# Second MLP product of token tiles 0 to 7 by seven block products in place of eight

## The chip, the cores and the metric

The kernel runs on one core of a Trainium2 chip. The core has a matrix engine (PE in the profile, with its weight loads shown apart as PEld), a vector engine (DVE), a scalar engine (ACT), a general engine (POOL, nearly idle here) and SP, whose queue issues most of the DMA transfers. Each engine works through its own instructions in the order in which the program lists them, and semaphores hold an instruction back until the instructions it depends on are done. The metric is the device time of one execution in microseconds; lower is better.

## What is computed

The reference normalises the 2048 tokens of x (512 features), sends them through an attention block with cached keys and values (32 heads of 128) and, beside it, through a gated MLP branch, and multiplies the two:

```python
xn = _layernorm(x, axis=-1)
s = _A_ref(xn, A_k_cache, A_v_cache, A_wq, A_wo)          # softmax attention, output projection
g = _silu(_B_ref(xn, B_w1, B_w2, B_w3, B_w4))
return x + s * g
# in _B_ref: hs = shifted gelu(layernorm(x) @ w1) @ w2;  x1 = x + hs
#            h2 = _gelu(_layernorm(x1) @ w3) @ w4;       return x1 + h2
```

The change concerns the last product alone, `gelu(...) @ w4`: 2048 tokens by 1792 hidden features, times 1792 by 512.

## The kernel before

All token work is in 16 tiles of 128 tokens. `xall` holds the running MLP state of all tiles in bf16, `h2T` the gelu output with the hidden features on the partitions, so that a block of 128 hidden features by 128 tokens can be a stationary operand as it lies.

The MLP branch runs first, in about the first 118 us; the attention loop over 128 units (head, quarter of the queries) follows and takes nearly all of the rest. Two functions carry the second MLP. `m3(c, f)` (line 286) makes two blocks of hidden features (f) for a chunk c of four token tiles: eight matmuls of 512 columns into a PSUM tile of two banks and one gelu on ACT over 1024 columns. `m4(t, ps, ...)` (line 295) makes the product of one token tile with `w4`: 14 matmuls of 512 columns, one for each block of hidden features, summed in one PSUM bank. `gate_out(t)` (line 815) wraps it: `m4`, then `x2` (line 301, DVE adds the bank to `xall`), `gate_tanh` (line 304, ACT) and `gate_silu` (line 309, DVE).

The order written out at lines 795 to 828 is: the 14 loads of `w4`, loads of the first keys and values mixed with `m3(0, ...)`, `m3(1, ...)` and the normalisations `ln2`, and then tiles 0 to 3 by `gate_out`, `m3(2, ...)`, tiles 4 to 7 by `gate_out`, `m3(3, ...)`. Tiles 8 to 15 (`held`, line 849) are worked off a few matmuls at a time inside the attention loop and are not touched by the change, beyond the names of their operands.

`pin` keeps every engine's instructions in the order of the text. On the SP queue the order around the change is: 14 loads of `w4` (line 796), keys and values of head 0, four transposes of `ln2(8)` to `ln2(11)`, keys and values of head 1, four transposes of `ln2(12)` to `ln2(15)` (line 284), keys and values of heads 2 and 3, four loads of `wo`.

Tiles of memory come from pools. A tag names a group of buffers of one size: `bufs=5` under tag `xi` means five of them, taken by each new tile in the order in which they came free; a new tile's first writer waits until all that read or wrote the buffer's last tile is done, transfers included. Line 171 takes from tag `xi`: for the input tiles 0 to 4, and in `ln2` for the normalised tiles with even t, which are read by the transposes of line 284:

```python
        y = token(t % 2 == 0, "xn2")
        norm_to(y[:], xall[:, t, :], mv2, rs2, t)
        pin(nc.sync.dma_start_transpose(out=xn2T[c][:, :, ts * P:(ts + 1) * P], in_=y[:]))
```

In PSUM, tag `ps_o` has two banks, `xa` and `xm` one each, and `ps_s` two tiles of two banks. Accesses of different engines to one PSUM tile are ordered by bank: a matmul that writes one half of a bank waits for an engine that reads the other half, and the other way round. The kernel has one block scheme of seven products already, for the queries (`product`, `q_take`, `q_part`, lines 367 to 423).

Of the kernel before, what the change touches and what calls it, by code (L numbers as in the profile page):

```python
# [8 lines left out]
ACT = mybir.ActivationFunctionType  # L9
ALU = mybir.AluOpType  # L10
FP32 = mybir.dt.float32
BF16 = mybir.dt.bfloat16
# [5 lines left out]
def kernel(  # L18
# [15 lines left out]
    nc = tc.nc  # L34
    P = nc.NUM_PARTITIONS
# [3 lines left out]
    Sq, D = x2d.shape  # L39
    _, H, Sk, Dh = A_k_cache.shape  # L40
# [5 lines left out]
    DC = D // P  # L46
    KC = Sk // P
    FC = F // P
# [11 lines left out]
    PADW = 8  # L60
    PSUM = bass.MemoryType.PSUM
    pin = tc.keep_in_program_order

    def pool(name, bufs=1, space=None, **kw):
        if space is not None:
            kw["space"] = space
        return tc.tile_pool(name=name, bufs=bufs, **kw)
# [4 lines left out]
    xall = const.tile([P, NT, D], BF16, name="xall")  # L72
# [22 lines left out]
    psO = ent(pool("psO", 2, PSUM))  # L95
    psX = ent(pool("psX", 1, PSUM))
# [4 lines left out]
    pR = right.enter_context(pool("pR", side="right", reuse_waits="tile"))  # L101
    left = ExitStack()
    pL = left.enter_context(pool("pL", reuse_waits="tile"))
# [7 lines left out]
    def mm(out, lhsT, rhs, start, stop, **kw):  # L111
        pin(nc.tensor.matmul(out=out, lhsT=lhsT, rhs=rhs, start=start, stop=stop, **kw))  # L112
# [8 lines left out]
        out=ident[:], in0=diag[:], scalar1=0.0, scalar2=None, op0=ALU.is_equal))  # L121
# [47 lines left out]
    def token(early, name):  # L169
        if early:  # L170
            return pL.tile([P, D], BF16, tag="xi", bufs=5, name=name)
        return tokp.tile([P, D], BF16, tag="ta", bufs=6, name=name)
# [9 lines left out]

    w1_sb = pL.tile([P, DC, D], BF16, name="w1_sb")
    w2_sb = pL.tile([P, DC, D], BF16, name="w2_sb")
    w3_sb = [pL.tile([P, DC, 2 * P], BF16, name=f"w3_sb{i}") for i in range(FC // 2)]
    hT = pL.tile([P, DC, Sq + PADW], BF16, name="hT")
    xn2T = {}
    w4_sb = [pR.tile([P, D], BF16, name=f"w4_sb{i}") for i in range(FC)]  # L190
    h2 = {}

    def power(out, ve):
# [92 lines left out]
    def m3(c, f):  # L286
        ps = psS.tile([P, 2, 512], FP32, name="ps_s")
        for j in range(2):
            for dc in range(DC):
                mm(ps[:, j, :], w3_sb[f][:, dc, j * P:(j + 1) * P], xn2T[c][:, dc, :],  # L290
                   dc == 0, dc == DC - 1)
        h2[c, f] = pR.tile([P, 2, 512], BF16, tag="h2T", bufs=FC, name="h2T")
        pin(nc.scalar.activation(out=h2[c, f][:], in_=ps[:], func=ACT.Gelu_apprx_tanh))  # L293

    def m4(t, ps, fcs):
        c, ts = divmod(t, 4)
        for fc in fcs:
            mm(ps[:], h2[c, fc // 2][:, fc % 2, ts * P:(ts + 1) * P], w4_sb[fc][:],
               fc == 0, fc == FC - 1)

    def x2(t, ps):
        pin(nc.vector.tensor_tensor(out=xall[:, t, :], in0=ps[:], in1=xall[:, t, :], op=ALU.add))

    def gate_tanh(t):
        th = token(False, "th")
        pin(nc.scalar.activation(out=th[:], in_=xall[:, t, :], func=ACT.Tanh, scale=0.5))
        return th

    def gate_silu(t, th):
        pin(nc.vector.scalar_tensor_tensor(  # L310
            out=xall[:, t, :], in0=th[:], scalar=1.0, in1=xall[:, t, :], op0=ALU.add, op1=ALU.mult))
# [29 lines left out]
    def x_block(qt, half, dcs):  # L341
        c = qt * 512 + 256 * half
        return xnT[:, dcs, c:c + 256]
# [23 lines left out]
    def product(v, k):  # L367
        g, qt, hh = units[v]
        h = g * HG + hh
        s = sw.setdefault(v, {})  # L370
        if k in (1, 7):
            s["ps"] = psX.tile([P, 2, 256], FP32, tag="xa", name="ps_q")
        w, o = wc[h], [wc[h][:, i] for i in range(4)]
        b11, _, b21, b22 = (wqs[h + j][:, d, :] for d in (LO, HI) for j in (0, 1))
        side, x, b = {
            1: (0, x_block(qt, 0, LO), b11),
            2: (0, x_block(qt, 0, HI), b21),
            3: (1, xs[qt, 3], b22),
            4: (0, x_block(qt, 1, HI), o[3]),
            5: (1, xs[qt, 0], o[0]),  # L380
            6: (1, xs[qt, 1], o[1]),
            7: (0, xs[qt, 2], o[2]),
        }[k]
        for dc in range(2):
            mm(s["ps"][:, side, :], b[:, dc, :], x[:, dc, :], k in (1, 7) and dc == 0, True, skip_group_check=True)
# [296 lines left out]
    for jc in range(DC):  # L682
        b = BASE_J[jc]
# [109 lines left out]
        elif t < 13:  # L793
            ln2(t - 5)
    for i in range(FC):
        pin(nc.sync.dma_start(out=w4_sb[i][:], in_=B_w4[i * P:(i + 1) * P, :]))
    for t in range(8, 12):
        stats(xall[:, t, :], mv2, rs2, t)
    for h in range(HG):
        load_k(h, range(KSPLIT))  # L800
        load_v(h, (0, 1))
        if h == 0:
            for f in range(FC // 2):
                m3(0, f)
            for t in range(12, 16):
                stats(xall[:, t, :], mv2, rs2, t)
            for t in range(8, 12):
                ln2(t)
        if h == 1:
            for f in range(FC // 2):  # L810
                m3(1, f)
            for t in range(12, 16):
                ln2(t)

    def gate_out(t):
        ps = psO.tile([P, D], FP32, tag="ps_o", name="ps_o")
        m4(t, ps, range(FC))
        x2(t, ps)
        gate_silu(t, gate_tanh(t))

    for t in range(0, 4):
        gate_out(t)
    for f in range(FC // 2):
        m3(2, f)
    for t in range(4, 8):
        gate_out(t)
    for f in range(FC // 2):
        m3(3, f)
    left.close()
    pB = left.enter_context(pool("pB", reuse_waits="tile"))  # L830

# [5 lines left out]
    for g in range(NG - 1):  # L837
        b = (g * QT + QT - 1) * HG
# [18 lines left out]
    def held_mm(n):  # L857
        for _ in range((4, 10)[n] if n < 2 else 3 if n < SPU + 2 else 2 if n < 2 * SPU else 1 + (n % SPU in (1, 5, 7))):
            if not held:
                return  # L860
            t, fc = held.popleft()
            if fc == 0:
                heldps[t] = psX.tile([P, 512], FP32, tag=("xa", "xm")[t % 2], name="ps_m")
            m4(t, heldps[t], (fc,))
            if fc == FC - 1:
                held_out(t, n)
# [34 lines left out]
    for v in pairs:  # L901
        a = (v - 2) * SPU
# [19 lines left out]
    for h in range(HG, H, 2):  # L922
        u = (h // HG) * QT * HG + (-4, -2)[h % HG // 2]
# [8 lines left out]
    for n in range(UB * SPU):  # L932
        u, p = divmod(n, SPU)
# [72 lines left out]
    n = UB * SPU  # L1006
    t0 = 4 * (QT - 1)
    ps, tb, yl, whole = {}, {}, {}, {}
# [25 lines left out]
    def pv_to(k):  # L1034
# [29 lines left out]
        out=diag[:], in0=diag[:], scalar1=0.0, scalar2=None, op0=ALU.is_equal))  # L1064
# [98 lines left out]
```

## Time and profile before

| | |
|---|---|
| median of 3 runs | 1236.7 us (1235.96 to 1236.73) |
| profiled execution | 1236.42 us, of which 1234.6 us from the first to the last instruction |
| PE busy | 1227.5 us of the span, 6267 matmuls |
| DVE busy | 1030.1 us, 1647 instructions |
| ACT busy | 1105.8 us, 1237 instructions |
| tiles 0 to 3 by `gate_out` | first matmul at 69.53 us |
| `m3(2, ...)` | first matmul at 81.62 us |
| tiles 4 to 7 by `gate_out` | first matmul at 93.70 us |
| `m3(3, ...)` | first matmul at 105.79 us |

The profiled execution is 0.28 us under the median. Times in the profile count from the first instruction. Matmuls are pipelined: one of 512 columns is listed with 379 ns, but in a row of them the next starts long before the last has ended, so that the cost of a stretch is read from the starts. In a group, "idle before" is the time that the engine stood before these instructions, with what ended most of it.

### The profile page before, as it was taken

Reading aid. Unit: us, or ns where it says so; the run is one execution under the profiler, and the core shown is the slowest. Engines: PE = TensorE matmul, PEld = TensorE weight load, DVE = VectorE, ACT = ScalarE, POOL = GpSimd, SP = SyncE. Lnnn points to the kernel's source line nnn. Section 1 sums busy time; section 2 is a strip of 40 time slices with the busy share of each in tenths; the row PEclk is TensorE's granted clock in tenths of the full one; section 3 lists DMA queues with packets and bytes.
Section 4 is the critical chain, followed back from the end, with each engine's and each line's share of the span. In section 5 each row is a group of like instructions: output and inputs, shape, how many; then the busy total and the mean of one; then the engine's idle time right before and its main releaser. Section 6 shows DMA issues by size and latency. Waiting matters only on the chain.

```text
span 1234.6 us, 17534 instructions
## 1 busy us (share of the span) xinstructions
PE 1227.5 (99%) x6267; PEld 636.5 (52%) x6267; DVE 1030.1 (83%) x1647; ACT 1105.8 (90%) x1237; POOL 26.6 (2%) x75
## 2 busy tenths in 40 slices
PE   9999999999999999999999999999999999999998
PEld 6444444455555555555555555555555555555545
DVE  7712778899888888988889888888889999999997
ACT  6345999899999999999999999999999999999996
POOL 5300000000000000000000000000000000000000
PEclk9999999999999999999999999999999999999999
DMA  8661122664334423354243523543345424553342
GB/s 176 168 140 35 31 39 65 96 99 94 63 80 100 106 57 82 87 111 85 58 95 91 111 56 69 103 104 72 76 83 111 107 58 90 99 107 66 77 81 66
DMA packets 244056, 107.75 MB, mean 87 GB/s; under 512 B 194816, under 2 KB 227712, under 8 KB 243968
## 3 DMA queue, kind: packets, MB, share of 16 engines
q1 hardware_dynamic: 243408, 106.17, 41.5%
q8 instruction: 49, 0.80, 0.3%
q10 hardware_dynamic: 560, 0.46, 0.1%
q14 instruction: 39, 0.32, 0.1%
HBM read 67.50 MB, written 2.36 MB: 57 GB/s over the span
## 4 chain that ended last, share of the span: by engine, by line
PE 94%; DVE 3%; DMA 2%; ACT 1%; issue 0%; SPq 0%; DVEq 0%; ACTq 0%
PE ps_s L112 39%; PE ps_o L112 37%; PE ps_wo L112 8%; PE ps_q L112 8%; PE ps_m L112 2%; DMA tT<-acc 1%; DVE acc L447 1%; ACT pT L436 1%; DMA rb<-dr 0%; DMA xin<-in_A_x_dram 0%; DVE sm L485 0%; PE ps_oh L112 0%; DVE oT L509 0%; DVE acc L451 0%; DVE y L1025 0%
## 5 line engine op out<-in xcount | busy, mean ns | idle before, releaser
L436 ACT ACTIVATE pT<-ps_s 128x1024 bf16<-128x1024 f32 x1016 | 1016.2, 1025 | 56.8 <-PE ps_s L112 26.1
L112 PE MATMUL ps_s<-qT,kT 128*128 128x512 bf16 (+1 forms) x2064 | 609.3, 378 | 0.0
L112 PE MATMUL ps_o<-pT,vb 128*128 128x512 bf16 x1984 | 590.2, 379 | 0.0
L447 DVE TENSOR_TENSOR acc<-acc,pT 128x2048 bf16<-128x2048 bf16 x254 | 307.0, 1208 | 54.9 <-ACT pT L436 54.4
L112 PEld LDWEIGHTS <-kT 128*128 128x128 bf16 x2064 | 232.7, 113 | 151.3 <-issue 1.0
L112 PEld LDWEIGHTS <-vb 128*128 128x128 bf16 x1984 | 193.9, 98 | 216.6
L442 DVE TENSOR_TENSOR acc<-pT 128x2048 bf16<-128x2048 bf16 x127 | 155.4, 1224 | 38.4 <-ACT pT L436 35.5
L112 PE MATMUL ps_wo<-wo_h,oT 128*128 128x512 bf16 x496 | 186.3, 379 | 0.0
L451 DVE TENSOR_TENSOR acc<-acc 128x1024 bf16<-128x1024 bf16 x127 | 87.4, 688 | 2.5
L509 DVE TENSOR_TENSOR oT<-ps_o,rb 128x512 bf16<-128x512 f32 x127 | 86.6, 682 | 1.1 <-DMA rb<-dr 0.8
L485 DVE TENSOR_REDUCE sm<-tT 128x4 f32<-128x512 bf16 x124 | 83.9, 676 | 2.8 <-DMA tT<-acc 2.7
L112 PEld LDWEIGHTS <-oT 128*128 128x128 bf16 x528 | 51.4, 98 | 52.6 <-issue 0.6
L112 PEld LDWEIGHTS <-wc 128*128 128x128 bf16 x440 | 43.0, 98 | 54.1 <-issue 2.7
L571 DVE TENSOR_TENSOR sacc<-ps_wo,sacc 128x512 f32<-128x512 f32 x96 | 65.7, 684 | 0.0
L112 PEld LDWEIGHTS <-wq_h 128*128 128x128 bf16 x398 | 38.9, 98 | 46.3
L112 PE MATMUL ps_q<-xnT,wq_h 128*128 128x256 bf16 (+1 forms) x288 | 61.1, 298 | 0.4 <-DVE sacc L559 0.4
L421 DVE TENSOR_TENSOR qT<-ps_q,tq 128x512 bf16<-128x512 f32 x55 | 38.0, 692 | 23.3 <-PE ps_q L112 22.9
L455 DVE TENSOR_TENSOR acc<-acc 128x512 bf16<-128x512 bf16 x127 | 52.9, 417 | 0.5
L293 ACT ACTIVATE h2T<-ps_s 128x1024 bf16<-128x1024 f32 x28 | 28.6, 1023 | 25.9 <-PE ps_s L112 25.9
L112 PE MATMUL ps_s<-xn2T,w_sb 128*128 128x512 bf16 x224 | 48.8, 379 | 0.0
L112 PEld LDWEIGHTS <-w_sb 128*128 128x128 bf16 x368 | 33.5, 98 | 29.6
L112 PE MATMUL ps_q<-xs,wc 128*128 128x256 bf16 x246 | 47.0, 273 | 0.0
(102 smaller groups left out, 585.6 us busy)
## 6 DMA issues: line engine op xcount, KB each, us to landing
rb<-dr SPq DMA_DIRECT2D x127, 256.0 KB, 3.9
vb<-in_A_v_cache_dram SPq DMA_DIRECT2D x62, 256.0 KB, 3.0
wq_h<-in_A_wq_dram SPq DMA_DIRECT2D x32, 128.0 KB, 3.0
wo_h<-in_A_wo_dram SPq DMA_DIRECT2D x32, 128.0 KB, 2.5
w_sb<-in_B_w_dram SPq DMA_DIRECT2D x8, 256.0 KB, 5.0
kT<-in_A_k_cache_dram SPq DMA_TRANSPOSE x128, 2.8
xl<-in_A_x_dram SPq DMA_DIRECT2D x16, 128.0 KB, 3.0
dr<-rc SPq DMA_DIRECT2D x127, 2.0 KB, 1.4
```

What stands on the lines that cost most here:

```text
L112: pin(nc.tensor.matmul(out=out, lhsT=lhsT, rhs=rhs, start=start, stop=stop, **kw))
L293: pin(nc.scalar.activation(out=h2[c, f][:], in_=ps[:], func=ACT.Gelu_apprx_tanh))
L421: pin(nc.vector.tensor_tensor(out=s["q"][:, 1:3], in0=ps, in1=u.to_broadcast([P, 2] + list(u.shape[2:])), op=ALU.add))
L436: pin(nc.scalar.activation(out=s["pT"][-1][:, jj:jj + 2, :], in_=sps[:], func=ACT.Exp, scale=SCALE))
L442: pin(nc.vector.tensor_tensor(out=s["acc"][:], in0=s["pT"][0][:], in1=s["pT"][1][:], op=ALU.add))
L447: pin(nc.vector.tensor_tensor(out=a[:], in0=a[:], in1=st[u]["pT"][i][:], op=ALU.add))
L451: pin(nc.vector.tensor_tensor(out=a[:, 0:2, :], in0=a[:, 0:2, :], in1=a[:, 2:4, :], op=ALU.add))
L455: pin(nc.vector.tensor_tensor(out=a[:, 0, :], in0=a[:, 0, :], in1=a[:, 1, :], op=ALU.add))
L485: pin(nc.vector.tensor_reduce(out=sm[:], in_=s["tT"][:], axis=mybir.AxisListType.X, op=ALU.add))
L509: pin(nc.vector.tensor_tensor(out=to, in0=o, in1=rb, op=ALU.mult))
L571: pin(nc.vector.tensor_tensor(out=sa, in0=ps[:], in1=sa, op=ALU.add))
```

## The change

For two token tiles at a time, the hidden features are split into even and odd blocks of 128 (seven each), the rows of `w4` with them, and the 512 output columns into halves. The product of a pair is then two by two blocks times two by two blocks, and these are multiplied by seven block products and sums of blocks (the Winograd form of Strassen's scheme). Each block product is seven matmuls of 256 columns. Four differences of blocks of `w4` are made once (`w4t`), four sums and differences of blocks of the hidden state for each pair (`h_sums`), both on DVE; `pair_out` holds the seven products and eight sums on the output side, one copy on ACT among them. `w4_sb` and `h2` become one tile each (per chunk), so that even and odd blocks can be addressed by one instruction.

The new tiles sit in buffers that earlier tiles have left: `w4t` in that of `hT`, the operand sums of a pair in the four buffers `xp` or in those of `w1` and `w2`, and the temporaries of 256 columns in the five buffers `xi`. The first pair of a chunk uses PSUM tag `xa` and the second `xm`; both use the two banks `ps_o`. The gates of a first pair are issued inside the second pair, behind its copy on ACT and ahead of its first sum on DVE.

```diff
-    w1_sb = pL.tile([P, DC, D], BF16, name="w1_sb")
-    w2_sb = pL.tile([P, DC, D], BF16, name="w2_sb")
+    w1_sb = pL.tile([P, DC, D], BF16, tag="w1", bufs=1, name="w1_sb")
+    w2_sb = pL.tile([P, DC, D], BF16, tag="w2", bufs=1, name="w2_sb")
...
-    hT = pL.tile([P, DC, Sq + PADW], BF16, name="hT")
+    hT = pL.tile([P, DC, Sq + PADW], BF16, tag="hT", bufs=1, name="hT")
...
-    w4_sb = [pR.tile([P, D], BF16, name=f"w4_sb{i}") for i in range(FC)]
+    w4_sb = pR.tile([P, FC // 2, 2, D], BF16, name="w4_sb")
...
-        h2[c, f] = pR.tile([P, 2, 512], BF16, tag="h2T", bufs=FC, name="h2T")
-        pin(nc.scalar.activation(out=h2[c, f][:], in_=ps[:], func=ACT.Gelu_apprx_tanh))
+        if f == 0:
+            h2[c] = pR.tile([P, FC // 2, 2, 512], BF16, tag="h2T", bufs=2, name="h2T")
+        pin(nc.scalar.activation(out=h2[c][:, f], in_=ps[:], func=ACT.Gelu_apprx_tanh))
...
-            mm(ps[:], h2[c, fc // 2][:, fc % 2, ts * P:(ts + 1) * P], w4_sb[fc][:],
+            mm(ps[:], h2[c][:, fc // 2, fc % 2, ts * P:(ts + 1) * P], w4_sb[:, fc // 2, fc % 2, :],
                fc == 0, fc == FC - 1)
...
-        pin(nc.sync.dma_start(out=w4_sb[i][:], in_=B_w4[i * P:(i + 1) * P, :]))
+        pin(nc.sync.dma_start(out=w4_sb[:, i // 2, i % 2, :], in_=B_w4[i * P:(i + 1) * P, :]))
...
-    for t in range(0, 4):
-        gate_out(t)
-    for f in range(FC // 2):
-        m3(2, f)
-    for t in range(4, 8):
-        gate_out(t)
-    for f in range(FC // 2):
-        m3(3, f)
+    w4t = pL.tile([P, 4, FC // 2, D // 2], BF16, tag="hT", bufs=1, name="w4t")
+    WL, WR = slice(0, D // 2), slice(D // 2, D)
+    b11, b12, b21, b22 = (w4_sb[:, :, k, c] for k in range(2) for c in (WL, WR))
+    t1, t2, t3, t4 = (w4t[:, i] for i in range(4))
+    for out, p, q in ((t1, b12, b11), (t2, b22, t1), (t3, b22, b12), (t4, b21, t2)):
+        pin(nc.vector.tensor_tensor(out=out, in0=p, in1=q, op=ALU.subtract))
+    hs = {}
+
+    def rows(t, k):
+        c, ts = divmod(t, 4)
+        return h2[c][:, :, k, ts * P:(ts + 1) * P]
+
+    def h_sums(t):
+        if t % 4 == 0:
+            hs[t] = [pL.tile([P, FC // 2, P], BF16, tag="xp", bufs=4, name="hs")[:] for _ in range(4)]
+        else:
+            two = [pL.tile([P, 2, FC // 2, P], BF16, tag=tag, bufs=1, name="hs") for tag in ("w1", "w2")]
+            hs[t] = [x[:, i] for x in two for i in range(2)]
+        s1, s2, s3, s4 = hs[t]
+        a11, a12, a21, a22 = (rows(t + r, k) for r in range(2) for k in range(2))
+        for out, p, q, op in ((s1, a21, a22, ALU.add), (s2, s1, a11, ALU.subtract),
+                              (s3, a11, a21, ALU.subtract), (s4, a12, s2, ALU.subtract)):
+            pin(nc.vector.tensor_tensor(out=out, in0=p, in1=q, op=op))
+
+    def flat(t, c0, n):
+        return xall[:].rearrange("p t d -> p (t d)")[:, t * D + c0:t * D + c0 + n]
+
+    def pair_out(t, between):
+        w = D // 2
+        s1, s2, s3, s4 = hs.pop(t)
+        a11, a12, _, a22 = (rows(t + r, k) for r in range(2) for k in range(2))
+        pa = psX.tile([P, 2, w], FP32, tag=("xa", "xm")[t % 4 // 2], name="ps_m")
+        pb, pc = (psO.tile([P, w], FP32, tag="ps_o", name="ps_o") for _ in range(2))
+
+        def product(out, a, b, start):
+            for f in range(FC // 2):
+                mm(out, a[:, f], b[:, f], start and f == 0, True, skip_group_check=True)
+
+        def tmp(n):
+            return pL.tile([P, n, w], FP32, **(dict(tag="xi", bufs=5) if n == 1 else dict(tag="mt", bufs=1)), name="mt")
+
+        def add(out, p, q):
+            pin(nc.vector.tensor_tensor(out=out, in0=p, in1=q, op=ALU.add))
+
+        m1c, u, u3, u3x, ux = tmp(1)[:, 0], tmp(1)[:, 0], tmp(1)[:, 0], tmp(1)[:, 0], tmp(2)
+        product(pa[:, 0], a11, b11, True)
+        pin(nc.scalar.activation(out=m1c, in_=pa[:, 0], func=ACT.Identity))
+        between()
+        product(pa[:, 1], s2, t2, False)
+        add(u, pa[:, 1], m1c)
+        product(pb[:], s3, t3, True)
+        add(ux[:], u.unsqueeze(1).broadcast_to([P, 2, w]), flat(t, w, 2 * w).rearrange("p (a c) -> p a c", a=2))
+        add(u3, pb[:], u)
+        product(pa[:, 0], a12, b21, False)
+        add(u3x, u3, flat(t + 1, w, w))
+        product(pc[:], s1, t1, True)
+        add(flat(t, 0, w), pa[:, 0], flat(t, 0, w))
+        add(flat(t + 1, w, w), pc[:], u3x)
+        product(pb[:], a22, t4, False)
+        product(pc[:], s4, b22, False)
+        add(flat(t + 1, 0, w), pb[:], ux[:, 1])
+        add(flat(t, w, w), pc[:], ux[:, 0])
+
+    def gate_pair(t):
+        th = [gate_tanh(t + i) for i in range(2)]
+        for i in range(2):
+            gate_silu(t + i, th[i])
+
+    for c in range(2):
+        h_sums(4 * c)
+        h_sums(4 * c + 2)
+        pair_out(4 * c, lambda: None)
+        pair_out(4 * c + 2, lambda: gate_pair(4 * c))
+        gate_pair(4 * c + 2)
+        for f in range(FC // 2):
+            m3(2 + c, f)
```

In the text below the seven products of a pair are called P1 to P7 in the order of `pair_out`, and the sums by the names of the code: m1c (on ACT), u, ux, u3, u3x, then C11 (from `pa`), C22 (`pc`), C21 (`pb`), C12 (`pc`), the last four into `xall`.

More of the change, by code (lines that the diff above doesn't have):

```diff
@@ L813 @@
                 ln2(t)
[L815 to L819, printed above, removed]
-    for t in range(0, 4):
-        gate_out(t)
-    for f in range(FC // 2):
-        m3(2, f)
-    for t in range(4, 8):
-        gate_out(t)
-    for f in range(FC // 2):
-        m3(3, f)
+    w4t = pL.tile([P, 4, FC // 2, D // 2], BF16, tag="hT", bufs=1, name="w4t")
+    WL, WR = slice(0, D // 2), slice(D // 2, D)
```

## The prediction

> **What bounds the kernel now.** I read the page from the top: the busy shares, the chain that ended last, then the stretch that the change touches by windows, by the chain in order of time and by the engines' timelines.
>
> ```profile
> span 1234.6 us, 17534 instructions
> PE 1227.5 (99%) x6267; PEld 636.5 (52%) x6267; DVE 1030.1 (83%) x1647; ACT 1105.8 (90%) x1237; POOL 26.6 (2%) x75
> PE 94%; DVE 3%; DMA 2%; ACT 1%; issue 0%; SPq 0%; DVEq 0%; ACTq 0%
> ```
>
> PE is busy all the time and makes 94% of the chain, so a microsecond of PE work saved, or of PE waiting added, should appear at the end in full. In the stretch itself (columns: length, then busy time of each engine with its instructions, clock, DMA share, GB/s):
>
> ```profile
> 69.50:81.60 12.10, 12.10 (x57) 5.49 (x56) 4.15 (x6) 2.91 (x4) 0.00 (x0) 1.00 0.80 127
> 93.70:105.80 12.10, 12.10 (x58) 5.47 (x57) 4.15 (x6) 2.91 (x4) 0.00 (x0) 1.00 0.22 71
> 69.69 12.09 PE ps_o L112 x56
> 81.78 12.09 PE ps_s L112 x56
> 93.87 12.09 PE ps_o L112 x56
> 69.53 12.25 PE L112 MATMUL ps_o<-w_sb,h2T 128*128 128x512 bf16 x56
> 81.62 2.75 PE L112 MATMUL ps_s<-xn2T,w_sb 128*128 128x512 bf16 x12
> 105.79 2.54 PE L112 MATMUL ps_s<-xn2T,w_sb 128*128 128x512 bf16 x11
> ```
>
> PE never stops there (12.10 of 12.10), while DVE has 4.15 us of work in 12.10 and ACT 2.91. The three lines of the chain say 12.09 us for 56 matmuls of 512 columns, 215.9 ns each; the timeline's starts (69.53, 81.62, 105.79) are the marks for what follows. Everything the change gives is PE time; everything it can lose is PE waiting for DVE and ACT, which are idle now but whose results PE will have to wait for.
>
> **The PE work.** A run of 256-column matmuls with a new weight each time is in the trace: 32 of them before the next group's start.
>
> ```profile
> 16.79 3.66 PE L112 MATMUL ps_s<-xnT,w_sb 128*128 128x256 bf16 x32
> 20.28 3.62 PE L112 MATMUL ps_q<-xnT,wq_h 128*128 128x512 bf16 x16
> ```
>
> (20.28 - 16.79) / 32 = 109.1 ns. A pair of tiles takes 28 x 215.9 = 6.05 us now and 49 x 109.1 = 5.35 us after, 0.76 us for each product. Four pairs: 2.8 us gained, 0.23% of the time. That is the ceiling, and only just over the 0.2% that a measurement of this kernel can tell from no change.
>
> [...]
>
> **Operand sums, loads, moves.** Four sums of 1792 columns and 16 of 896, bf16, on DVE. Rows, the first two with strided operands like the new ones:
>
> ```profile
> L365 DVE TENSOR_TENSOR wc<-wq_h 128x256 bf16<-128x256 bf16 x8 | 2.3, 284 | 0.0
> L356 DVE TENSOR_TENSOR xs<-xnT 128x512 bf16<-128x512 bf16 x5 | 2.1, 419 | 0.0
> L451 DVE TENSOR_TENSOR acc<-acc 128x1024 bf16<-128x1024 bf16 x31 | 21.4, 689 | 0.8
> 47.14 9.02 SPq L796 DMA_DIRECT2D w_sb<-in_B_w_dram  x14
> 92.74 1.89 SPq L516 DMA_DIRECT2D wo_h<-in_A_wo_dram  x4
> 131.28 1.23 SPq L480 DMA_TRANSPOSE tT<-acc  x1
> w_sb<-in_B_w_dram SPq DMA_DIRECT2D x1, 128.0 KB, 2.5
> 72.75 0.69 DVE L302 TENSOR_TENSOR xall<-ps_o,xall 128x512 bf16<-128x512 f32 x1 [17.32 <-PE ps_o L112]
> ```
>
> On their line (150 ns + 0.526 per column) 896 columns take 0.62 us and 1792 take 1.09 us: 4.4 us for `w4t`, 2.5 us for each pair. The last load of w4 is issued by 56.2 and lands 2.5 us later, 58.7; DVE stands idle from 55.4 to 72.75; `w4t` and eight sums end near 68, and PE wants the first, s2, for P2 after 70.3. The sums of tiles 4 to 7 come after the second pair's gates and lie under `m3(2)`, 12.09 us. So I cost them at nothing. Without the cover (slow operands, late w4) they would cost up to their own 9 us in the first chunk. The w4 loads keep their place and number on SP. The four wo loads, now at 92.74, would wait for the last pair's operands, whose buffers they take; the next SP issue is at 131 us, so nothing stands behind them that matters.
>
> **Output sums: a chain that runs beside PE.** The durations:
>
> ```profile
> L405 ACT ACTIVATE tq<-ps_q x55: 392/392/405, 248.1 to 1172.0; 128x256 f32<-128x256 f32 x55
> L413 DVE TENSOR_TENSOR tq<-ps_q,tq x55: 416/417/421, 251.1 to 1175.5; 128x256 f32<-128x256 f32 x55
> L421 DVE TENSOR_TENSOR qT<-ps_q,tq x55: 685/692/693, 261.9 to 1185.9; 128x512 bf16<-128x512 f32 x55
> L306 ACT ACTIVATE th<-xall 128x512 bf16<-128x512 bf16 x16 | 10.0, 626 | 19.8 <-DVE xall L302 19.8
> 69.73 1.02 ACT L293 ACTIVATE h2T<-ps_s 128x1024 bf16<-128x1024 f32 x1 [0.70 <-PE ps_s L112]
> L112 PE MATMUL ps_q<-xs,wc x246: 272/273/273, 249.6 to 1181.1; 128*128 128x256 bf16 x123
> ```
>
> So m1c 0.39 us, sums of 256 columns 0.42, ux (512) 0.69, tanh 0.63, silu 0.69 like x2; a product's result is there 0.16 us after its last issue slot (273 - 109 ns), and I add 0.03 to 0.05 us for each hand-over. All times below count from the pair's P1.
>
> Half-bank wait: P2 writes the bank that m1c reads, so it waits for m1c, as the query scheme's right half already does; there two steps of the loop lie between and hide it. Bounds: nothing if the halves were free, the whole wait if not; I take the whole.
> First pair of a chunk: the last gelu of `m3` holds ACT until 1.2 (69.73 + 1.02 against 69.53), m1c 1.25 to 1.64, P2 1.69 to 2.45, u to 3.06, ux to 3.75, u3 to 4.17, u3x to 4.59, C11 to 5.01, C22 to 5.43; P3 to P6 run through to 5.51, P7 needs C22 and ends at 6.27. That is 0.92 us over 5.35.
> Second pair: the first pair's gates stand ahead of u on DVE. m1c 0.96 to 1.35, then two tanh to 2.63, the second silu ends at 3.41, u 3.83, so P4 starts at 3.88; ux 4.52, u3 4.94, u3x 5.36, C11 5.78, C22 6.20, P7 6.25 to 7.01: 1.66 us over.
> The second pair's own gates lie under `m3`.
>
> **The wait that decides: a buffer of u3x.** `xi` has five buffers, taken in the order they come free: inputs 0 to 4, then `xn2` 0, 2, 4, 6, 8, then 10, 12, 14 on the first three again. The first pair asks for four: m1c gets that of 6, u that of 8, u3 that of 10, and u3x that of 12. Token tile 12 is read by its transpose on the SP queue, which stands behind the keys and values of head 1:
>
> ```profile
> 67.83 5.16 SPq L144 DMA_TRANSPOSE kT<-in_A_k_cache_dram  x4
> 73.04 1.09 SPq L160 DMA_DIRECT2D vb<-in_A_v_cache_dram  x2
> 74.24 5.85 SPq L284 DMA_TRANSPOSE xn2T<-xn  x4
> 77.57 1.22 SPq L284 DMA_TRANSPOSE xn2T<-xn  x1
> DMA to landing us min/median/max: 2.5/3.5/5.1
> xn2T<-xn SPq DMA_TRANSPOSE x1, 5.1
> xn2T<-xn SPq DMA_TRANSPOSE x1, 2.7
> 242.42 2.03 SPq L480 DMA_TRANSPOSE tT<-acc  x1
> tT<-acc SPq DMA_TRANSPOSE x1, 6.0
> 248.43 0.69 DVE L485 TENSOR_REDUCE sm<-tT 128x4 f32<-128x512 bf16 x1 [0.43 <-DMA tT<-acc]
> ```
>
> (The 5.1 is from the window 74 to 75 us, the 2.7, that of tile 14, from 77.5 to 78.6; the last three lines show that landing counts from the issue's start: 242.42 + 6.0 = 248.42, and the reader goes at 248.43.) Today nobody near waits for it: `m3(3)` wants it at 105.8. After the change u3x writes its buffer, so it can't start before 74.24 + 5.1 = 79.34, that is 9.87 after the pair's start at 69.53. Queued behind it on DVE are C11, C22, C21 and C12; P7 overwrites the bank that C22 reads, and the whole of PE stands behind P7. u3x to 10.29, C11 10.71, C22 11.13, P7 11.18 to 11.94: 6.59 us over 5.35, the 0.92 included. Tile 14's transpose (77.57 + 2.7 = 80.3) has landed when the second pair's m1c takes its buffer at 82.4. The second chunk finds all buffers free.
> Bounds for this landing: 2.5 us, the quickest of the four transposes (the line of minimum, median and maximum), to 6.0, the slowest quoted; net 5.4 to 8.9 us over today. I take 5.1, the same transfer's own.
>
> **Sum.** Pairs: 11.94 + 7.01 + 6.27 + 7.01 = 32.23 us against 4 x 6.05 = 24.18: 8.05 us more. On the profiled execution's 1236.42 us that gives 1244.5; its time is 0.28 us under the median, so on 1236.7 it is 1244.7.
>
> **Rivals.**
> Cold array. PE would stand from 5.51 to 11.18, 5.7 us, which this trace shows nowhere after the start. At the start it shows what a long rest leaves:
>
> ```profile
> 2.00:3.00 1.00, 1.00 (x13) 1.00 (x11) 0.00 (x0) 0.99 (x2) 0.00 (x0) 1.00 0.93 289
> 7.00:8.00 1.00, 1.00 (x22) 1.00 (x20) 1.00 (x3) 0.56 (x2) 0.74 (x3) 1.00 1.18 267
> PE ps_q L112 <- DVE qT L418: 1.4, 3, 1.0
> ```
>
> 13 matmuls of 128 columns in a microsecond, later 22, though the clock column says 1.00 in both. If P7 and the next pair's P1 run at 13/22 speed, each costs 0.5 us more on the path, the later products hide behind DVE's gates: +1.1, 1245.8; if it lasts into `m3(2)`, up to +2.5. Against it: PE's waits in the loop (the last line: three, the longest 1.0 us) are followed by pairs at full speed; but they are short.
> [...]
> No shared buffer. If u3x gets another buffer than tile 12's (m1c's, say, come free first), the first pair costs 6.27: +2.4 us, 1239.1. For it: the order of release is a matter of the schedule; against it: m1c is free only after u.
> DVE and ACT keep up (the other side). If neither the buffer, nor the half banks, nor the gates hold PE, the 2.8 us stay: 1233.9. It decides from less than 0.3 us of PE waiting in all four pairs; the second pairs alone have 1.66 us each by the order of the text, so this is unlikely.
> Late operands. If the sums run at the 1.05 ns per column of 32-bit ones, or w4 is waited for, the first chunk's sums end some 7 us later. Most of that lies under the wait for tile 12; beyond it 2 to 4 us: about 1248.
> Weight loads set the pace. From a spacing of 6.05 / 49 = 123 ns the 2.8 us are gone, and the time is 1247.5. The 109.1 ns above, with a new weight for every matmul, speak against it. [...]
>
> **How the numbers follow.** Forecast 0.52, cold array 0.26, no shared buffer 0.12 (its 1239.1 lies at the edge of 0.2%, 1239.2, so two thirds of it inside), late operands 0.06, DVE and ACT keep up 0.03, weight loads 0.01. Faster 0.03, within 0.2% 0.08, slower 0.89. The range goes from the no-shared-buffer case, 1239.0, to the bounds of the landing and of the cold array, 1247.5.
>
> **What would show it.** In the profile after: DVE idle some 5 us before u3x, released by the transpose of `xn` near 79.3; PE idle 5 to 6 us once, before the products into `pc`, and 1 to 2 us in each second pair; `m3(2)` starting near 88.5 and `m3(3)` near 113.9 in place of 81.62 and 105.79; after that the same kernel, shifted. I am wrong if `m3(2)` starts before 84, or if PE's waits stand before P1 (operands) and not before P7.

## The result and the profile after

The changed kernel takes 1243.3 us, median of six runs (1242.54 to 1246.28), against 1236.49 us for the kernel before, median of six beside them. The ratio is 1.0061, 95% interval 1.0049 to 1.0074: 6.8 us slower. Predicted were 1244.7 us, with 1239.0 to 1247.5 as the range.

The profiled execution is the slowest of the six, 1246.28 us. First the lines of its page that answer to those of before: the span, the busy times, the chain that ended last by engine.

```profile
span 1244.2 us, 17640 instructions
PE 1222.5 (98%) x6234; PEld 646.6 (52%) x6351; DVE 1051.2 (84%) x1691; ACT 1106.6 (89%) x1241; POOL 26.9 (2%) x75
PE 93%; DVE 3%; DMA 2%; issue 1%; ACT 0%; SPq 0%; DVEq 0%; ACTq 0%
```

PE's work is not what grew: it is busy 1222.5 us, 5 us less than before. (117 of the 6351 matmuls have no record in this trace, so that figure is a little low.) The span is 9.6 us longer, so PE stands idle somewhere. Where it stands idle is shown by the waits between 60 and 126 us (us in total, times, longest) and by the timelines of PE, DVE and SP (start, length, and in brackets the idle time before with its releaser):

```profile
DVE mt L858 <- DMA xn2T<-xn: 5.7, 1, 5.7
PE ps_o L112 <- DVE xall L858: 5.4, 1, 5.4
PE ps_m L112 <- ACT mt L862: 2.2, 4, 0.6
PE ps_m L112 <- DVE mt L858: 0.7, 2, 0.5
```

```profile
70.10 0.93 PE L112 MATMUL ps_m<-w_sb,h2T 128*128 128x256 bf16 x7
...
74.70 0.93 PE L112 MATMUL ps_o<-w4t,h2T 128*128 128x256 bf16 x7
81.04 1.65 PE L112 MATMUL ps_o<-w_sb,hs 128*128 128x256 bf16 x7 [5.42 <-DVE xall L858]
82.49 1.70 PE L112 MATMUL ps_m<-w_sb,h2T 128*128 128x256 bf16 x7
...
89.89 12.25 PE L112 MATMUL ps_s<-xn2T,w_sb 128*128 128x512 bf16 x54
```

```profile
73.73 0.42 DVE L858 TENSOR_TENSOR mt<-ps_o,mt 128x256 f32<-128x256 f32 x1
79.90 0.42 DVE L858 TENSOR_TENSOR mt<-mt,xall 128x256 f32<-128x256 f32 x1 [5.75 <-DMA xn2T<-xn]
```

```profile
74.57 5.92 SPq L284 DMA_TRANSPOSE xn2T<-xn  x4
```

The one large stop is the predicted one. DVE's sum `u3` is done at 74.15. The next, `u3x`, waits 5.75 us for a transpose of `xn` that SP issued at 74.57; P7, the last product of the first pair, waits 5.42 us for the sums behind it. `m3(2)` starts at 89.89 where it started at 81.62.

The table gives, for every kernel below, the start of the first product, the length of the four pairs (from a pair's first matmul to the next thing that PE begins), the span from `m3(3)` to its end, and the median less that of the kernel before on the same chip. Before, two pairs took 12.09 us together and the rest 1128.8.

| kernel | first product | pair 1 | pair 2 | pair 3 | pair 4 | `m3(3)` to end | median less before |
|---|---|---|---|---|---|---|---|
| changed | 70.10 | 12.39 | 7.40 | 6.13 | 6.64 | 1129.4 | +6.8 |
| changed, again | 69.64 | 10.60 | 7.40 | 6.13 | 6.64 | 1128.4 | +7.3 |
| changed, third | 69.62 | 11.40 | 7.40 | 6.13 | 6.64 | 1128.3 | +7.1 |
| own buffer | 69.62 | 6.13 | 6.64 | 6.46 | 6.63 | 1128.2 | +2.0 |
| buffer, split banks | 69.66 | 5.35 | 6.53 | 5.58 | 6.53 | 1128.5 | +0.1 |
| buffer, later gates | 69.57 | 6.13 | 5.99 | 6.13 | 5.98 | 1128.2 | +0.2 |
| all three | 69.43 | 5.35 | 5.35 | 5.35 | 5.35 | 1128.1 | -2.6 |
| transposes late | 69.73 | 17.42 | 7.44 | 6.13 | 6.63 | 1127.8 | +13.3 |
| transposes first | 69.84 | 6.13 | 6.63 | 6.13 | 6.63 | 1128.1 | +0.9 |
| gap filled, 24 | 69.67 | 11.31 | 6.64 | 6.14 | 6.63 | 1126.9 | +5.0 |
| gap filled, 19 | 69.79 | 10.23 | 6.64 | 6.14 | 6.63 | 1127.8 | +5.1 |

The first profile is unlucky in three places at once: against the third profile of the same kernel its first product comes 0.5 us later, its pair 1 is 1.0 us longer and its rest 1.1 us. The third profile belongs to an execution of 1243.33 us, the median, and is used below to settle the prediction term by term.

### The profile page after: what moved, and what is told of

The parts are those of the page before. It is cut to its first block, busy times and chain, and to the rows that moved or that the text cites. A ratio compares the mean times of both kernels' runs of the same rounds, so it can differ in the third digit from the quotient of the medians.

```text
span 1244.2 us, 17640 instructions
## 1 busy us (share of the span) xinstructions
PE 1222.5 (98%) x6234; PEld 646.6 (52%) x6351; DVE 1051.2 (84%) x1691; ACT 1106.6 (89%) x1241; POOL 26.9 (2%) x75
## 4 chain that ended last, share of the span: by engine, by line
PE 93%; DVE 3%; DMA 2%; issue 1%; ACT 0%; SPq 0%; DVEq 0%; ACTq 0%
PE ps_s L112 39%; PE ps_o L112 35%; PE ps_q L112 8%; PE ps_wo L112 8%; PE ps_m L112 3%; DMA tT<-acc 1%; DVE acc L448 1%; DMA rb<-dr 0%; DMA xn2T<-xn 0%; DMA xin<-in_A_x_dram 0%; DVE sm L486 0%; PE ps_oh L112 0%; DVE xall L311 0%; DVE oT L510 0%; DVE y L1088 0%
## 5 line engine op out<-in xcount | busy, mean ns | idle before, releaser
L112 PE MATMUL ps_o<-pT,vb 128*128 128x512 bf16 x1908 | 573.5, 379 | 3.2
L112 PE MATMUL ps_wo<-wo_h,oT 128*128 128x512 bf16 x475 | 178.2, 379 | 0.1
```

## Experiments: which part costs what

The theory under test is the prediction's: a buffer that one sum shares with token tile 12 costs most; the half-bank wait in first pairs and the gates ahead of the sums in second pairs cost the rest, and without them the 2.8 us of PE work appear. Four kernels take these away, one at a time and then together, all run on one chip beside a kernel before of 1235.77 us (33 runs).

**The buffer alone.** Token tiles 12 and 14 are normalised into buffers of the other tag, so that no sum takes theirs.

```diff
-        y = token(t % 2 == 0, "xn2")
+        y = token(t % 2 == 0 and t < 12, "xn2")
```

> Edit to the changed kernel: the normalised tiles 12 and 14 go to the other group of token buffers, so that no buffer of tag xi is still read by a late transpose when the first pair asks for its temporaries. Nothing else is touched. Theory A (the wait for tile 12's transpose is the bulk of the loss): u3x follows u3 at once, the first pair takes 6.1 us in place of about 11.7, PE has no gap over 1 us, and the time is 1237.9 us, 1.4 over before (pairs of 6.13, 6.64, 6.13, 6.64 us against 6.05 each). Rival B (PE would be held at that place anyhow, by the DVE chain or by the transfers of the keys that run then): the time stays at 1243.

Measured: 1237.81 us, ratio 1.0018 (1.0009 to 1.0027). PE's waits between 60 and 126 us are now these, and `m3(2)` starts 7.5 us earlier than in the changed kernel's first profile:

```profile
PE ps_m L112 <- ACT mt L862: 2.2, 4, 0.6
PE ps_m L112 <- DVE mt L858: 1.1, 3, 0.5
```

```profile
82.39 12.25 PE L112 MATMUL ps_s<-xn2T,w_sb 128*128 128x512 bf16 x56
```

One buffer carries 5 of the 7 us. The wait for the transpose is gone, and with it the length of pair 2 falls from 7.40 to 6.64, though nothing in pair 2 was touched. What that is, the last group of runs shows. Pair 3 is 0.33 us longer here than in the changed kernel: `u` began late on DVE, with no releaser that the profile shows, and this stays unexplained.

**The banks.** On top of it, the first and second product go to two PSUM banks in place of two halves of one, so that P2 need not wait for the copy `m1c`.

```diff
-        pa = psX.tile([P, 2, w], FP32, tag=("xa", "xm")[t % 4 // 2], name="ps_m")
+        pa = [psX.tile([P, w], FP32, tag=tag, name="ps_m")[:] for tag in ("xa", "xm")]
...
-        product(pa[:, 1], s2, t2, False)
+        product(pa[1], s2, t2, True)
```

> As e1, and the two halves of pa become tiles in two banks, xa and xm, for every pair, so that P2 does not wait for the copy m1c and P4 not for u. Theory A (the half-bank wait costs 0.62 us in every pair, and in the second pairs the gates take its place): first pairs 5.4 us, second pairs 6.5, because u still stands behind the gates and P6 waits for u3: 1236.1 us. Rival B (matmuls of 256 columns with operands from the new tiles are simply slower than 109 ns in this stretch): no change against e1, 1237.9.

Measured: 1235.89 us, ratio 1.0001 (0.9992 to 1.001). Pair 1 takes 5.35 us, the bare 49 matmuls. Pair 2 still takes 6.53, but now waits elsewhere, before P6 and P7:

```profile
79.65 0.92 PE L112 MATMUL ps_o<-w4t,h2T 128*128 128x256 bf16 x7 [0.66 <-DVE mt L858]
80.78 0.92 PE L112 MATMUL ps_o<-w_sb,hs 128*128 128x256 bf16 x7 [0.20 <-DVE xall L858]
```

The half-bank wait was real; in second pairs, removing it only lets PE run up against the sums that stand behind the gates.

**The gates.** On top of the buffer alone: inside a second pair only the two tanh of the first pair are issued; its two silu on DVE follow after the second pair's last sum.

```diff
-        pair_out(4 * c + 2, lambda: gate_pair(4 * c))
-        gate_pair(4 * c + 2)
+        pair_out(4 * c + 2, lambda: gate_tanhs(4 * c))
+        gate_silus(4 * c)
+        gate_tanhs(4 * c + 2)
+        gate_silus(4 * c + 2)
```

> As e1, and of the first pair's gates only the tanh on ACT stays inside the second pair; the two gate products on DVE come behind the second pair's last sum. Theory A (the order on DVE, not its amount of work, costs the second pairs their extra): second pairs 6.0 us like the first without the gelu ahead, 1236.5 us. Rival B (DVE has too much work in these stretches, some 3.6 us of sums and 1.3 of gates in a pair): moving the gates gains nothing, or the sums of the next chunk come late and PE waits before P2 of tile 4: 1237.9 or more.

Measured: 1235.98 us, ratio 1.0004 (0.9995 to 1.0013). Second pairs fall from 6.64 to 5.99, and PE's only waits in the stretch are the four for `m1c`:

```profile
PE ps_m L112 <- ACT mt L862: 2.2, 4, 0.6
```

**All three together.**

> e1, e2 and e3 together: no shared buffer, two banks, gate products behind the second pair. Theory A (the three waits are all that stands between the change and its ceiling): four pairs of 5.35 us, 2.8 us under before, 1233.7 us. Rival B (something else takes their place: PE waiting for pb or pc, or for the operand sums): between 1234.5 and 1236.5, with PE waits in the stretch that name it.

Measured: 1233.18 us (1232.82 to 1234.24), ratio 0.998 (0.9972 to 0.9989): faster than both kernels. The windows of the two chunks (length, then busy time of PE and its matmuls, PEld, DVE, ACT, POOL, clock, DMA share, GB/s) show PE without a stop:

```profile
69.43:80.13 10.70, 10.70 (x99) 9.60 (x98) 6.43 (x15) 2.72 (x5) 0.00 (x0) 1.00 0.71 133
92.22:102.92 10.70, 10.70 (x100) 9.59 (x99) 6.44 (x15) 2.72 (x5) 0.00 (x0) 1.00 0.19 56
```

Two pairs take 10.70 us where eight block products took 12.09: 2.78 us less in all, 2.59 in the medians. The idea of the change is worth what its matmuls say, as soon as nothing else holds them. The two waits do not add: from the buffer alone, the banks bring 1.9 us and the gates 1.8, both together 4.6, because in a second pair each of them hides behind the other.

## Experiments: is it that transpose

If `u3x` waits for the transpose of tile 12 and for nothing else, the wait must move with the transpose. Two kernels keep the buffers as in the changed kernel and move only the four `ln2` of tiles 12 to 15, their transposes with them; a third is the changed kernel again. The kernel before on this chip took 1236.3 us (15 runs).

Behind the values of head 2:

```diff
+        if h == 2:
             for t in range(12, 16):
                 ln2(t)
```

> Edit to the changed kernel: the four transposes of tiles 12 to 15 are issued behind the keys and values of head 2 in place of ahead of them, 6.3 us later on the SP queue (four transposes of keys in 5.17 us and two loads of values in 1.09). Buffers as in the changed kernel. Theory A (u3x waits for tile 12's transpose): the wait grows by the same 6.3 us, u3x starts near 86, and the time is 1243.3 + 6.3 = 1249.6 us. Rival B (the wait is for something else at that time, such as the values of head 1 or the DVE chain): the time stays at 1243.

Measured: 1249.56 us, ratio 1.0108 (1.0095 to 1.0122). The transposes are issued 6.5 us later than in the changed kernel's first profile, and PE's wait is 10.4 us in place of 5.4. It grew by 5.0 us there and not by the 6.3 expected, since the transpose took 3.45 us from its issue to the sum (81.11 to 84.56) in place of 5.33 (74.57 to 79.90); that the time is the expected one to 0.1 us is in part luck.

```profile
81.11 5.16 SPq L284 DMA_TRANSPOSE xn2T<-xn  x4
```

```profile
84.56 0.42 DVE L859 TENSOR_TENSOR mt<-mt,xall 128x256 f32<-128x256 f32 x1 [10.78 <-DMA xn2T<-xn]
```

Ahead of the keys of head 1:

```diff
+        if h == 1:
+            for t in range(12, 16):
+                ln2(t)
         load_k(h, range(KSPLIT))
```

> Edit to the changed kernel: the four transposes are issued ahead of the keys and values of head 1. u3x still takes tile 12's buffer. Theory A (the place in the queue, not the buffer as such, makes the wait): tile 12's transpose is issued when m3 of chunk 1 has ended, near 70, and has landed near 73, before u3x is ready near 73.7; the time is that of the kernel without the shared buffer, 1237.8 us. Rival B (any buffer last read by a transfer costs the wait, or the later keys cost as much elsewhere): above 1240.

Measured: 1237.2 us, ratio 1.0008 (0.9999 to 1.0017). No loads of keys stand between the eight transposes now. The group below has a pause in it: the last four leave from 70.03 on, when `m3(1)` has read the tile that they write. `u3x` follows `u3` at once, and no sum waits for a transpose:

```profile
61.49 13.66 SPq L284 DMA_TRANSPOSE xn2T<-xn  x8
```

```profile
73.47 0.42 DVE L859 TENSOR_TENSOR mt<-ps_o,mt 128x256 f32<-128x256 f32 x1
73.92 0.43 DVE L859 TENSOR_TENSOR mt<-mt,xall 128x256 f32<-128x256 f32 x1
```

```profile
82.60 12.25 PE L112 MATMUL ps_s<-xn2T,w_sb 128*128 128x512 bf16 x56
```

So with the same shared buffer the kernel is 13 us, 7 us or 1 us slower than the kernel before, by where one transfer stands in SP's queue. In the last 1 us the buffer has no part: pair 1 takes 6.13 us, as with its own buffer, and what is left are the waits at the half bank and behind the gates. That the buffer and the queue together make the wait is shown from both sides, without touching the sums.

The changed kernel again:

> The changed kernel itself again, on the same chip and beside the same runs of before, for its spread: its six runs lay between 1242.5 and 1246.3 us. Theory A (a slower array after the gap in some executions): the profile shows P7 and the product after it either at 1.5 to 1.65 us or at 0.93, and the runs spread over 1.5 us or more, where those of the kernels without the gap spread over 1.0 to 1.6. Rival B: the first profile was a disturbed one, and all runs lie within 1 us.

Measured: 1243.58 us, ratio 1.006 (1.0047 to 1.0073); `u3x` started 1.9 us earlier than in the first profile (78.00 against 79.90), so P7 waited 3.97 us.

## Experiments: what the stop leaves behind

In the first profile P7 took 1.45 us to the start of the next product (81.04 to 82.49), where a product takes 0.76, and that next one 1.70 with its tail, where the others have 0.93. Two kernels fill the stop with matmuls between P6 and P7, on an unused PSUM tile; nobody reads them, so they are extra work and change nothing that is computed. If the slow products come from the stop, they must go.

```diff
         product(pb[:], a22, t4, False)
+        if t == 0:
+            fill = psS.tile([P, 2, 512], FP32, name="ps_s")
+            for i in range(24):
+                mm(fill[:, i % 2, :], a11[:, 0], w4_sb[:, 0, 0, :], True, True)
         product(pc[:], s4, b22, False)
```

> Edit to the changed kernel: 24 matmuls of 512 columns, 5.2 us, whose result nobody reads, stand between the sixth and the seventh product of the first pair, where PE has nothing to do for 5.4 us. Theory A (after the gap the array runs slower for some time, as the 1.65 us of P7 and 1.51 of the next product in the profile say, against 0.76): all products take 0.76 us again, the second pair takes 6.64 us, and the time falls to the lower end of the changed kernel's runs, 1242.5 us, with less spread. Rival B (the slow products come from the transfers of the keys and values that run at the same time): P7 and the next product stay at 1.5 us, and the time stays or rises.

Measured: 1241.25 us (1241.20 to 1241.39), ratio 1.0041 (1.0027 to 1.0055), 2.3 us under the changed kernel on the same chip and 1.2 us under the expected 1242.5, although the 24 matmuls ended about 1 us after `u3x` would have let P7 go (`u3x` started at 78.02, and P7, 1.15 us behind it in the changed kernel, started at 80.22). With 19 in place of 24, and the changed kernel a third time beside it (kernel before: 1236.22 us):

> As in the run with 24 filler matmuls, but with 19, which by that run's 5.34 us for 24 (0.2225 us each) take about 4.2 us and end before the running sum u3x where its transpose lands after 79.2. The seventh product of the first pair then waits for u3x alone, on an array that has just worked. Theory (the gap leaves the array at half rate, and this costs 1.1 to 1.45 us in the changed kernel): seventh product 0.76 us from its first matmul to that of the next product, second pair 6.64 us, and since the 24 fillers overran the wait by about 1.1 us at worst and by nothing where the transpose came late, a time from 1240.2 to 1241.3, 2.3 to 3.3 us under the changed kernel on the same chip. Rival (the 2.3 us by which the 24 fillers were faster came mostly from something else in the kernel, and the half rate is a mark with little cost): products as above, but a time within 1 us of the changed kernel's 1243.4.

> The changed kernel itself, beside the filled one on the same chip. Every theory: 1243.4 within 0.6 us; its first pair 10.6 to 12.4 us by when the transpose of token tile 12 lands, its seventh product 1.1 to 1.5 us, its second pair 7.40.

Measured: 1241.32 us (ratio 1.0043, 1.0029 to 1.0057) with 19, and 1243.33 us (1.0056, 1.0042 to 1.007) for the changed kernel. PE with 19 fillers, then PE in the changed kernel, then the DVE sum `u3x` in the changed kernel and with 19 fillers:

```profile
75.16 4.26 PE L112 MATMUL ps_s<-w_sb,h2T 128*128 128x512 bf16 x19
79.26 0.93 PE L112 MATMUL ps_o<-w_sb,hs 128*128 128x256 bf16 x7
80.02 0.93 PE L112 MATMUL ps_m<-w_sb,h2T 128*128 128x256 bf16 x7
81.42 0.93 PE L112 MATMUL ps_m<-w4t,hs 128*128 128x256 bf16 x7 [0.47 <-ACT mt L862]
```

```profile
69.62 0.93 PE L112 MATMUL ps_m<-w_sb,h2T 128*128 128x256 bf16 x7
...
79.89 1.34 PE L112 MATMUL ps_o<-w_sb,hs 128*128 128x256 bf16 x7 [4.74 <-DVE xall L858]
81.02 1.70 PE L112 MATMUL ps_m<-w_sb,h2T 128*128 128x256 bf16 x7
83.19 1.14 PE L112 MATMUL ps_m<-w4t,hs 128*128 128x256 bf16 x7 [0.47 <-ACT mt L862]
...
88.42 12.25 PE L112 MATMUL ps_s<-xn2T,w_sb 128*128 128x512 bf16 x56
```

```profile
78.74 0.43 DVE L858 TENSOR_TENSOR mt<-mt,xall 128x256 f32<-128x256 f32 x1 [5.07 <-DMA xn2T<-xn]
77.95 0.42 DVE L858 TENSOR_TENSOR mt<-mt,xall 128x256 f32<-128x256 f32 x1 [4.10 <-DMA xn2T<-xn]
```

With the stop filled, P7 takes 0.76 us to the start of the next product again (79.26 to 80.02), and pair 2 takes 6.64 us. The granted clock reads 1.00 in every stretch from 76.00 to 90.00 with 19 fillers and from 75.00 to 87.60 with 24, where it falls to 0.50 in the changed kernel (last section); the slow stretch is called the half rate below. With the stop, P7 takes 1.13 (to 81.02) and the next product 1.70 with its tail against 0.93; pair 2 is 0.76 us longer. In the profiles the half rate thus costs 0.37 + 0.76 = 1.1 us here and 0.69 + 0.76 = 1.45 in the first profile. The transfers of the keys and values run in the filled kernels as well (with 19, the next transposes of keys are issued from 79.63 on, and the DMA share from 80 to 82 is 0.41 against 0.37 in the third profile), so they are not what makes the products slow.

The medians differ by 2.0 and 2.3, and these differences are not the price of the half rate. With 19 fillers pairs 1 and 2 are 1.93 us shorter than in the third profile, but 0.80 of that is P7 starting earlier, because `u3x` came 8.16 us after the pair's start in place of 9.12. With 24, pairs 1 and 2 together take 17.95 us against 18.00 in the second profile of the changed kernel; the 1.5 us between their spans lie in the part from `m3(3)` to the end (1126.9 against 1128.4), which the fillers don't explain. So the price rests on the lengths of the products, 1.1 to 1.45 us; what else the fillers did to the medians is open.

## Why the prediction held

The mechanism was right at the three places the forecast named, the buffer, the half bank and the gates, and the sum was 0.7 us too large against the third profile (four pairs: 32.23 predicted, 31.57 measured). That closeness is partly luck: the pairs were put 1.8 us too long, and 1.1 us of half rate was left out.

- **PE work.** 109.1 ns for a matmul of 256 columns: right. Without waits a pair takes 5.35 us, as said, and the ceiling of 2.8 us came out at 2.78. Against the 6.05 us of two token tiles before, a pair of the all-three kernel is 0.70 us cheaper.
- **Operand sums at no cost.** Right: 0.62 and 1.09 us each, the last one of the first chunk ended at 67.1 in the first profile, and none of PE's waits is for one:

```profile
66.49 0.62 DVE L838 TENSOR_TENSOR hs<-h2T,hs 128x896 bf16<-128x896 bf16 x1
```

- **The buffer.** Right in cause and place. `u3x` was put at 9.87 after the pair's start and came at 9.12 in the third profile, 9.80 in the first, 8.36 in the second. The landing was well put: 5.29, 5.33 and 4.84 us from the issue to the sum, against 5.1. What varied more is the issue, put at 4.71 after the pair's start (74.24) and measured at 3.83, 4.47 and 3.52; in the third profile:

```profile
73.45 6.05 SPq L284 DMA_TRANSPOSE xn2T<-xn  x4
```

From `u3x` to P7 I had 1.31 us; it was 1.15. Without the half rate, pair 1 would have been 11.03, against 11.94.
- **First pair of the second chunk.** 6.27 predicted, 6.13 measured: P2 started 1.55 after P1 and not 1.69, since ACT's copy starts before the gelu ahead of it has quite ended (103.10 against 103.20 in the first profile).
- **Second pairs.** 7.01 predicted, 6.64 measured. With 19 fillers the first silu began 1.90 after P1 (81.92), where the working gives 2.03, and from there to `u` the two silu took 1.21 us (to 83.13) and not 1.38, because the second starts before the first has ended (1.29 us for the two, 0.69 for one alone). So `u` began 3.11 after P1 and not 3.41, and P7 then ran straight behind P6, where I had it wait for the sum C22.
- **The cold array.** What the prediction had wrong is the weight between the forecast and this rival. I gave 0.52 to a full-rate P7 and 0.26 to a slow one; the slow one happened, in each of the four profiles with a stop and no fillers. Its size was well put in total: +1.1 us by my rows at the start of the kernel; 1.1 to 1.45 was measured. The parts were not: P7 and P1 were put at 0.5 us each and cost 0.37 and 0.76 in the third profile, since the drop came when P7 had begun. The rate of 13/22 was misread too, because such a row counts a matmul in every microsecond that it touches (the rows of 1 to 2 and 2 to 3 us count 10 and 13, one row from 0.97 to 3.00 counts 20). By starts, the trace of the kernel before has 20 matmuls in its first 2.03 us of PE work, 107 ns each, and later 16 in 0.89 us (6.92 to 7.81), 56 ns each: half. The clock column was no help there. It says 1.00 over those slow first matmuls, which no run here explains, while behind the stop of the first profile it reads 0.50 where P7 takes 1.45 us in place of 0.76; so 1.00 at the start was no evidence against the effect. I read those first matmuls as what a rest leaves; no run varied what stands ahead of them. In none of the four profiles did the half rate last into `m3(2)`, the case put at up to +2.5 us: in the first it ended near 85.26, and `m3(2)` started at 89.89.
- **No shared buffer, late operands, weight loads, and no wait at all** did not occur. The kernel with its own buffer, where the buffer's wait is gone by design, came out 2.0 us over the kernel before; that rival's sum had 2.4, by the same oversized pairs.

The predicted 1244.7 was the sum without the half rate; with the pairs as the third profile has them, half rate included, the same sum gives 1236.2 + 7.39 = 1243.6, measured 1243.33.

## What to carry to other kernels

When a change takes scratch space from a group of buffers, list for every new tile the last reader of the buffer that it gets, transfers included, and when that reader is done: a reader that nobody waited for before becomes part of the path, and its place in a DMA queue sets the price (here the kernel was 1, 7 or 13 us slower than before, with the sums unchanged). Before calling a scheme with less PE work a loss, look for its waits one by one and remove them together; two that cover each other show less than their worth alone (1.9 and 1.8 us here, 4.6 together). And expect slow matmuls behind a stop of PE such as the four here, of 3.97 to 10.44 us: each had them, and in the changed kernel they cost 1.1 to 1.45 us.

## What the runs showed of the hardware

In the four profiles with a stop and no fillers the clock falls to 0.50 for a while. Clock column (the number third from the end of each line) of the changed kernel's first profile, of the second, of the third, and of the kernel with late transposes:

```profile
78.00:79.00 1.00, 0.00 (x0) 0.00 (x0) 0.00 (x0) 0.00 (x0) 0.00 (x0) 0.72 0.07 10
79.00:85.00 6.00, 3.48 (x16) 2.27 (x16) 1.85 (x5) 0.78 (x2) 0.00 (x0) 0.50 0.60 125
85.00:86.00 1.00, 1.00 (x10) 0.83 (x8) 0.84 (x2) 0.64 (x2) 0.00 (x0) 0.87 0.36 63
```

```profile
79.00:80.00 1.00, 0.86 (x6) 0.69 (x6) 0.42 (x2) 0.00 (x0) 0.00 (x0) 0.77 0.45 89
80.00:82.00 2.00, 1.94 (x10) 1.22 (x8) 0.42 (x1) 0.03 (x1) 0.00 (x0) 0.50 0.50 113
82.00:83.00 1.00, 0.59 (x4) 0.42 (x4) 0.09 (x1) 1.00 (x3) 0.00 (x0) 0.52 0.27 57
```

```profile
80.00:81.00 1.00, 1.00 (x7) 0.75 (x6) 0.16 (x1) 0.00 (x0) 0.00 (x0) 0.62 0.18 38
81.00:83.00 2.00, 1.72 (x9) 1.06 (x7) 0.42 (x1) 0.24 (x1) 0.00 (x0) 0.50 0.56 126
83.00:84.00 1.00, 0.81 (x6) 0.65 (x6) 0.31 (x1) 1.00 (x3) 0.00 (x0) 0.67 0.40 92
```

```profile
80.00:81.00 1.00, 0.00 (x0) 0.00 (x0) 0.00 (x0) 0.00 (x0) 0.00 (x0) 0.77 0.58 129
81.00:90.00 9.00, 3.83 (x18) 2.56 (x18) 2.03 (x6) 1.11 (x3) 0.00 (x0) 0.50 0.62 146
90.00:91.00 1.00, 1.00 (x8) 0.71 (x7) 1.00 (x2) 0.30 (x1) 0.00 (x0) 0.61 0.57 130
```

In the first profile the column reads 1.00 from 75.50 to 78.40, 0.50 from 78.45 to 85.25 and 1.00 from 85.27 to 95.00. If the clock is either 1.00 or 0.50 in the other three as well, a microsecond with 0.72 holds 0.56 us of the half rate (twice what is missing from 1.00). The stretches then last 6.82, 3.42, 3.42 and 10.24 us: two, one, one and three times 3.41; what sets that length no run here shows. In the third profile the drop comes at 80.24, after P7 has begun at 79.89, and in the second at 79.54, after 79.14, so these two stops were paid for when they were already over. The length of the stop mattered little for the price: behind the stop of 10.44 us P7 and pair 2 cost 0.69 + 0.80 = 1.5 us, behind that of 5.42 us 1.45, behind those of 3.97 and 4.74 us 1.1. The difference lies in P7, which ran slowly from its first matmul in the first two and was caught by the drop on its way in the others.

The same transpose of one tile took 4.84 to 5.33 us from its issue to the sum that waits for it in three profiles of the changed kernel, and 3.45 in the kernel with late transposes: here the landing read at one place in the queue did not hold at the other.
